# Batch 0's first row half multiplied unfolded, and its scores in two tiles: a chunked attention followed by a Fourier mixing layer on one core

## The chip, the core and the metric

The kernel runs on one core of one Trainium2 chip. The metric is the device time of one execution in microseconds (us). Three runs of the kernel before took 282.17, 284.47 and 280.91, median 282.17. A separate, profiled execution is what all views of the profile below come from.

## The reference

Two layers, for 4 batches of 768 positions, 8 heads of 64 (512 columns):

```python
for c in range(nc):                               # chunks of 32 queries
    k_ctx = k[:, :, l_start:r_end]                # 16 keys to the left, 8 to the right
    k_full = np.concatenate([mem_k, k_ctx], axis=2)   # and 8 memory keys; v alike
    scores = scale * np.matmul(q_c, k_full.transpose(0, 1, 3, 2))
    a = softmax(scores)
    out[:, :, c_start:c_end] = np.matmul(a, v_full)
x = out.transpose(0, 2, 1, 3).reshape(B, S, H * D)
mixed = np.real(fft(fft(x, axis=1), axis=2))      # over 768 positions, then 512 columns
u = x + mixed
un = (u - mean(u)) / sqrt(var(u) + 1e-06)
return u + np.maximum(un @ w_ch1, 0.0) @ w_ch2    # 512 -> 2048 -> 512
```

`softmax` stands here for the reference's maximum, exponential and division.

## The kernel before

**Who orders the work.** The program is a list of tasks. Each `add(engine, cost, emit, after, take, give, ...)` names an engine, a cost in us, the tasks it comes after and the buffers it takes and gives back. `Plan.order()` walks a clock of its own over this list, picks for each engine the first task in rank whose conditions hold, and emits the instructions in that order. The order is thus fixed when the program is built; on the chip each engine works strictly in it and waits on semaphores. While the first scores are due, the planner puts small matmuls on a zero tile (`idle`, L902) where it sees TensorE without work; until `WARM` it counts TensorE's costs double.

**Attention.** A pair of heads is one unit n; `seq` gives 4 pairs for each of 4 batches (n = 0 to 15). For each n, GpSimd's queue loads queries and keys into one of three stages (`qs`, `ks`, L349; for batch 3 L345), SP's queue loads the values in seven pieces into one of four tiles `va` (L358, L362, L367). TensorE turns queries and keys (`trq`, `trk`, L377, 16 matmuls each), ScalarE copies the turned queries (L395), VectorE in batch 0 and ScalarE later copies the keys into `kTb` (L420), and TensorE computes scores in two halves g = 0, 1 of 12 matmuls (`sc`, L433). All score halves share one PSUM tile `sc`: the second half can be computed when ScalarE's exponential of the first (L441, two instructions, into one of three tiles `e`) has read it. The value products follow (`xa`, `xo`, L457), with the softmax sum as a column of their own, and VectorE divides into `xsb` (L467, L468). The first 32 rows of each `va` are zeroed on ScalarE (L331, 1.5 us each). A copy named `gate` (L956, GpSimd) reads a value of the last pair of batch 0, second head, and thereby holds the loads of batch 1 behind that transfer.

**Fourier layer.** It is a product with cosine and sine tables. Rows first: the columns are folded so that only sums and differences are multiplied. For batches 1 to 3 (`fourier`, L529) all six row tiles come at once. For batch 0 (`first_fourier`) the work is done in two row halves g: g = 0 as soon as the first three row tiles of all four pairs are there. VectorE adds and subtracts column halves (`zy`, L599), folds them twice (`ff`, L610, for g = 0; `g_w` and `g_both`, L616 and L635, for g = 1), ScalarE rounds to f16 (`hi`, L651), VectorE takes the remainder (`lo`, L655), and TensorE multiplies with the tables (`ps`, L688, 12 matmuls for each of four column parts (par, ab) and each half). One column that the folding leaves over is multiplied by itself (`mid`, L675, after a matmul with zeros, L669, that opens its tile). Each finished part is copied by ScalarE and VectorE in two f16 pieces (`up`, L541, L546). Then the column products (`pm`, L699), the sum with the input (L705), mean and variance (L713, L714), the normalised tile (`un`), its turn (`tp`, L730, in batch 0) and the two layers.

**Layers.** `ph` (L775) is layer 1, in groups of 8 matmuls, with the relu on ScalarE (L784). `pc` (L793) is layer 2 for batches 0 and 1, and L842 with half the width, with fewer products, for batches 2 and 3. The weights come on GpSimd's queue (`w_sb`, L1062 for layer 1, L1067 for layer 2). TensorE's order interleaves the layers of one batch with the attention of the next.

PSUM: tags `acc` and `mlp` have two banks each, `tr`, `sc` and `xa` one each.

Of the kernel before, what the change touches and what calls it, by code (L numbers as in the profile page):

```python
# [10 lines left out]
FP32 = mybir.dt.float32  # L11
BF16 = mybir.dt.bfloat16
# [24 lines left out]
class Plan:  # L37
# [4 lines left out]
    LAG = {"PE": 0.2}  # L42
    FIRST = 45.0
    WARM = 18.0
    SLACK = 0.7
    FILL = 0.17
# [44 lines left out]

    def order(self):
        now, idle = 0.0, {}
        self.flow, self.seen = {}, 0.0
# [6 lines left out]
        placed = []  # L101
        while any(waiting.values()):
# [5 lines left out]
            for e, ts_ in waiting.items():  # L108
                if idle.get(e, 0.0) > now:
                    continue  # L110
                held = False
                for t in ts_:
# [29 lines left out]
                    idle[e] = t["end"] = now + cost  # L142
                    if t["moved"]:
                        self.flow.setdefault(e, []).append([t, t["moved"], now + cost * t["head"]])
                        self.share(now)
                        t["end"] = t["done"]
                    else:
# [10 lines left out]
                else:  # L158
                    if e == "PE" and self.filling and self.filling[0]["at"] is not None \
                            and self.filling[1]["at"] is None:  # L160
                        cost = self.FILL * (2.0 if now < self.WARM else 1.0)
                        idle[e] = now + cost
                        placed.append(dict(engine="PE", cost=cost, emit=self.fill, at=now,
                                           done=now + cost))
                        moved = True
            if not moved:
                times = ([v for v in idle.values() if v > now] + [g[0] for g in gives]
                         + [t["done"] + x for t in placed for x in (0.0, self.SLACK, 4.0, 8.0)
# [9 lines left out]
def kernel(  # L178
# [38 lines left out]

    bank_of, bank_free = {}, {"acc": [0, 1], "mlp": [0, 1]}

    def bank(tag, shape, dtype, name):  # L220
        i = bank_free[tag].pop(0)
        t = fps.tile(shape, dtype, tag=f"{tag}{i}", bufs=1, name=name)
# [14 lines left out]
    ks = [spool.tile([P, 2, RB * D], BF16, name=f"ks{i}") for i in range(NS)]  # L237
    NV = 4
# [43 lines left out]
    odd = wpool.tile([P, 2, 3, NK], FP16)  # L282
    cosD = wpool.tile([P, 2, HD], FP16)
# [45 lines left out]
    def e_low_rows(i):  # L329
        low = va[i][0:MEM0].rearrange("p h t c -> p (h t c)")  # L330
        nc.scalar.copy(low, zero[0:MEM0].to_broadcast([MEM0, 2 * NT * 66]))  # L331
# [8 lines left out]
    def e_load_qk(n, i):  # L340
        b, pr = seq[n]
        src, dst = ((q, qs), (k, ks))[i]
        if b >= TURNED:
            for hh in range(2):
                nc.gpsimd.dma_start(  # L345
                    strided(dst[n % NS], hh * D, [[2 * D, NST], [1, D]]),
                    src[b, 2 * pr + hh].rearrange("(a p) d -> p a d", p=P))
            return
        nc.gpsimd.dma_start(dst[n % NS][0:QP],  # L349
# [30 lines left out]
    def e_flip_q(n):  # L380
        qT_of[n] = qT = apool.tile([P, S], BF16, tag="qT", bufs=2, name="qT")
        nc.sync.dma_start_transpose(qT.rearrange("p (a s) -> p a s", s=P),
                                    qs[n % NS].rearrange("p h c -> p (h c)")[:, 0:S])

    def e_flip_k(n):
        nc.sync.dma_start_transpose(kU[n % NKU][:, KR:KR + S].rearrange("p (a s) -> p a s", s=P),
                                    ks[n % NS].rearrange("p h c -> p (h c)")[:, 0:S])
# [1014 lines left out]
```

## Time and profile before

| what | value |
|---|---|
| profiled execution, own time | 282.55 us |
| its span | 280.7 us |
| median of the three runs | 282.17 us |
| TensorE busy | 264.3 us (94%) |
| VectorE, ScalarE, GpSimd busy | 193.5, 155.2, 64.3 us |
| granted TensorE clock | 1.00 throughout |
| share of the chain that ended last | TensorE 84%, DMA 7%, VectorE 4%, SP's queue 3% |
| first layer-1 matmul | at 57.1 us |
| last TensorE instruction ends | at 277.5 us |

The page gives busy times by engine, and the span in 40 slices whose digits are tenths of busy time. PE is TensorE, PEld its weight loads, DVE is VectorE, ACT ScalarE, POOL GpSimd, SP the queue that issues most transfers. L numbers are lines of the kernel. In a timeline each row has the start, the duration, the engine, the line, the operation, and in brackets the idle time before it with what ended it. Matmuls overlap each other, so that a row's duration is longer than the step from one to the next; steps are read from start to start.

### The profile page before, as it was taken

The numbers are of one execution on the slowest core, as the hardware profiler recorded it, in microseconds if no ns is written. First come the engines' busy times: TensorE is split into PE (matmuls) and PEld (weight loads), VectorE is DVE, ScalarE is ACT, GpSimd is POOL, SyncE is SP. The second block draws the span as 40 slices with busy tenths as digits, with TensorE's granted clock in tenths as the row PEclk, the third lists the DMA queues.
The fourth block names the chain that finished last, engine by engine and source line by source line (L and its number), as shares of the span: only waits on it lengthen the run. The fifth ranks groups of instructions, "written<-read, shape, count | busy, mean of one in ns | idle before, by whom it ended". The sixth has DMA issues, their size and how long they took to land.

```text
span 280.7 us, 7981 instructions
## 1 busy us (share of the span) xinstructions
PE 264.3 (94%) x3325; PEld 207.4 (74%) x3325; DVE 193.5 (69%) x424; ACT 155.2 (55%) x262; POOL 64.3 (23%) x127
## 2 busy tenths in 40 slices
PE   0589999999999999998999999999999999999995
PEld 0466698788756579766668766858988888888884
DVE  7968978970218979899688776599869825353444
ACT  6887667579665757734745665525526270605150
POOL 8840853240111038306200230101004100000000
PEclk9999999999999999999999999999999999999999
DMA  6989999999899969999999734497101507103152
GB/s 102 199 143 174 162 206 204 196 198 201 162 190 236 214 103 220 177 142 144 235 191 209 177 74 109 108 207 167 48 37 58 131 21 168 40 37 77 50 103 76
DMA packets 116116, 39.98 MB, mean 142 GB/s; under 512 B 104560, under 2 KB 111472, under 8 KB 116080
## 3 DMA queue, kind: packets, MB, share of 16 engines
q1 hardware_dynamic: 93888, 23.54, 46.9%
q0 software_dynamic: 21472, 15.21, 34.0%
q10 hardware_dynamic: 720, 0.72, 0.7%
q8 instruction: 26, 0.43, 0.7%
q14 instruction: 10, 0.08, 0.1%
HBM read 37.36 MB, written 13.37 MB: 181 GB/s over the span
## 4 chain that ended last, share of the span: by engine, by line
PE 84%; DMA 7%; DVE 4%; SPq 3%; issue 1%; POOL 0%; POOLq 0%
PE ph L775 31%; PE pc L793 15%; PE pc L842 13%; DMA va<-in_v_dram 6%; PE ps L529 6%; PE xa L457 4%; PE pm L699 4%; PE ps L688 3%; PE xo L457 3%; PE sc L433 2%; SPq L358 2%; DMA qs<-in_q_dram 1%; PE trk L377 1%; PE trq L377 1%; DVE xsb L705 1%; PE pm L580 1%
## 5 line engine op out<-in xcount | busy, mean ns | idle before, releaser
L775 PE MATMUL ph<-unT,w_sb 128*128 128x256 f16 x768 | 90.3, 273 | 0.8 <-DVE xsb L800 0.8
L784 ACT ACTIVATE hT<-ph 128x512 f16<-128x512 f32 x96 | 56.9, 598 | 54.3 <-PE pc L842 30.2
L775 PEld LDWEIGHTS <-w_sb 128*128 128x128 f16 x768 | 73.2, 98 | 11.1 <-issue 1.7
L793 PE MATMUL pc<-w_sb,hT 128*128 128x512 f16 x192 | 44.8, 380 | 0.0
L441 ACT ACTIVATE e<-sc,mbias 128x384 f32<-128x384 f32 x64 | 33.6, 576 | 19.0 <-PE sc L433 19.0
L793 PEld LDWEIGHTS <-hT 128*128 128x128 f16 x192 | 17.7, 98 | 19.0 <-issue 0.2
L847 DVE TENSOR_TENSOR xsb<-pc,xsb 128x256 f32<-128x256 f32 x43 | 18.0, 421 | 12.4 <-PE pc L842 10.6
L842 PEld LDWEIGHTS <-hT 128*128 128x128 f16 x240 | 23.3, 98 | 4.2 <-DVE hT L830 1.0
L842 PE MATMUL pc<-w_sb,hT 128*128 128x256 f16 x192 | 24.1, 272 | 0.5 <-DVE hT L830 0.5
L541 ACT CAST up<-ps 128x386 f16<-128x386 f32 x16 | 9.7, 605 | 17.6 <-PE ps L529 17.0
L830 DVE TENSOR_TENSOR S<-hT 128x768 f16<-128x768 f16 (+1 forms) x12 | 5.1, 422 | 18.5 <-ACT hT L784 17.9
L800 DVE SCALAR_TENSOR_TENSOR xsb<-pc,rstd,xsb 128x512 f32<-128x512 f32 x12 | 9.0, 750 | 12.2 <-PE pc L793 12.1
L713 DVE BATCH_NORM_STATS2 st<-xsb 128x6 f32<-128x512 f32 x24 | 16.6, 690 | 0.6
L705 DVE TENSOR_TENSOR xsb<-pm,xsb 128x512 f32<-128x512 f32 x15 | 10.2, 678 | 7.1 <-PE pm L699 6.9
L457 PEld LDWEIGHTS xa<-va,e 128*64 128x64 f32 x384 | 12.5, 137 | 3.2 <-issue 2.0
L457 PE MATMUL xa<-va,e 128*64 128x65 f32 x384 | 14.7, 226 | 0.0
L433 PEld LDWEIGHTS <-kTb 64*128 64x128 bf16 x384 | 7.8, 96 | 9.0 <-issue 8.1
L457 PE MATMUL xo<-va,e 128*64 128x65 f32 x384 | 14.1, 223 | 0.0
L546 DVE TENSOR_TENSOR up<-ps,up 128x386 f16<-128x386 f32 x16 | 9.6, 602 | 6.1 <-ACT up L541 6.1
L395 ACT COPY qT<-trq 128x768 bf16<-128x768 bf16 x12 | 9.5, 793 | 6.4 <-PE trq L377 6.4
L572 POOL DMA_DIRECT2D xr<-x_back x3 | 2.3, 770 | 46.7 <-DMA x_back<-x_rows 46.7
L519 DVE TENSOR_TENSOR lo<-ff,hi 128x768 f16<-128x768 f32 x12 | 11.3, 954 | 2.4 <-ACT hi L514 2.4
(168 smaller groups left out, 455.3 us busy)
## 6 DMA issues: line engine op xcount, KB each, us to landing
va<-in_v_dram SPq DMA_DIRECT2D x32, 220.0 KB
w_sb<-in_moe_w_ch_dram POOLq DMA_DIRECT2D x8, 512.0 KB, 16.9
out_dram<-xsb SPq DMA_DIRECT2D x12, 256.0 KB
qs<-in_q_dram POOLq DMA_DIRECT2D x12, 192.0 KB, 6.5
ks<-in_k_dram POOLq DMA_DIRECT2D x12, 192.0 KB, 7.0
x_rows<-xsb POOLq DMA_DIRECT2D x3, 768.0 KB, 4.6
xr<-x_back POOLq DMA_DIRECT2D x3, 768.0 KB, 5.0
out_rows<-xsb SPq DMA_DIRECT2D x9, 256.0 KB
```

The costliest lines, as they stand in the source:

```text
L433: nc.tensor.matmul(sc[:, hh, t6, :], kT[r0:r0 + 64, t, :], qT[r0:r0 + 64, ts(t, 64)], start=True, stop=True, tile_position=(r0, 0))
L441: nc.scalar.activation(e1[:, :, :, ts(half, 32)], sc[:, :, 0:6, ts(half, 32)], AFT.Exp, bias=mbias[:, half:half + 1], scale=1.0 / math.sqr ...
L457: nc.tensor.matmul(xa[64 * half:64 * half + 64, st, hh, 0:65], e1[:, hh, t6, :], v1[:, hh, 6 * g + t6, 0:65], start=True, stop=True)
L519: nc.vector.tensor_tensor(lo[:, ab].rearrange(fl), ff_of[b, par][:, ab].rearrange(fl), hi[:, ab].rearrange(fl), ALU.subtract)
L529: nc.tensor.matmul(out_[:, sp, :], part[:, ab, sp * 3 + st, c0:c1], tab[:, sp, st, :], start=(st == 0 and i == 0), stop=(st == 2 and i == 1))
L705: nc.vector.tensor_tensor(uv, pm_of[b, kt], uv, ALU.add)
L713: nc.vector.bn_stats(st6, xs[b][:, kt, :])
L775: nc.tensor.matmul(ph[:, k, :], w1_sb[:, dt, ts(HH * k + i, P)], unT_of[b, j][:, dt, :], start=(dt == 0), stop=(dt == NDT - 1))
L784: nc.scalar.activation(hT_of[b, j][:, :, i, :], ph, AFT.Relu, bias=0.0, scale=1.0 if b in EVEN else -1.0)
L793: nc.tensor.matmul(pc_of[b, j, r], hT_of[b, j][:, k, i, ts(r, P)], w2_sb[:, HH * k + i, :], start=(i + k == 0), stop=(i + k == HH))
L842: nc.tensor.matmul(pc_of[key], a[:, i, :], w[:, i, :], start=(i == 0 and new), stop=(i == HH - 1), skip_group_check=not new)
L847: nc.vector.tensor_tensor(u, pc, u, ALU.add)
```

## The change

Batch 0's first row half (g = 0) is no longer folded at the second level. Its column half `zy` and a reversed half (`g_back`) are each rounded and multiplied (`g_rows0`, two passes `back` = 0, 1), the second pass partly with negated tables (`odd`, and `neg`, new, in the buffer `S`). The second half (g = 1) stays folded and is added to the same PSUM sums; the left-over column of both halves is combined on GpSimd and multiplied once at the end (`g_mid`, `g_row`). The score tile of g = 1 in batch 0 is half of a new two-bank tile `accs` from a pool that is given back before the first `acc` bank is used; two of the four row sums sit in the `sc` tile. The fourth pair has a stage of its own (`last_qk`). Two of the `va` tiles are zeroed on GpSimd. The planner's costs are changed, `WARM` is 6, its filling matmuls use any of three tags and give them back, and it makes 24 orders with randomly moved ranks and keeps the one that ends first by its own clock. Values of n = 14, 15 are issued after the turned rows of batch 2; layer 2's weights go out after n = 7. Keys of n = 5, 6, 7 are copied by VectorE.

```diff
-    WARM = 18.0
+    OVER = {"DVE": 0.08, "ACT": 0.1}
+    WARM = 6.0
+    ROOM = 2.2
...
+    def shortest(self, tries, spread):
+        ...
+        for i in list(range(tries)) + [None]:
+            draw = random.Random(found[1] if i is None else i)
+            ...
+            for t, rank in zip(self.tasks, ranks):
+                move = draw.gauss(0.0, spread)
+                t["rank"] = rank if even or rank < self.lead or rank > 1e5 else rank + move
...
+            placed = self.order()
+            if found is None or self.end < found[0]:
+                found = (self.end, i)
+        return placed
...
+                        tag = next((x for x in ("mlp", "tr", "xa") if self.free[x] > 0), None)
...
+    early = tc.tile_pool(name="early_ps", bufs=1, space=bass.MemoryType.PSUM)
+    accs = [early, early.__enter__().tile([P, 2, 512], FP32, name="accs")]
...
+        if tag == "acc":
+            if len(accs) == 2:
+                early.__exit__(None, None, None)
...
+    last_qk = wpool.tile([P, 2, 2, RB * D], BF16, tag="w2t", bufs=1, name="last_qk")
...
+    neg = fpool.tile([P, 2, 3, NK], FP16, tag="S", bufs=1, name="neg")
...
-        nc.scalar.copy(low, zero[0:MEM0].to_broadcast([MEM0, 2 * NT * 66]))
+        if i < 2:
+            nc.scalar.copy(low, zero[0:MEM0].to_broadcast([MEM0, 2 * NT * 66]))
+        else:
+            nc.gpsimd.memset(low, 0.0)
...
+    KDVE, QDVE = (5, 6, 7), ()
...
-        if n < HP:
-            trk = bank("acc", [P, RB * KP], BF16, "trk")
+        tr_of[n, 1] = trk = (bank("mlp", [P, RB * KP], BF16, "trk") if n < HP else
...
-        sc_of[n, g] = sc = aps.tile([P, 2, 8, 64], FP32, tag="sc", bufs=1, name="sc")
+        sc_of[n, g] = sc = (accs[1].rearrange("p h (t q) -> p h t q", q=64) if n < HP and g == 1 else
+                            aps.tile([P, 2, 8, 64], FP32, tag="sc", bufs=1, name="sc"))
...
-    def g_ff(par, ab, g, last):
...
+    def g_back(par):
+        ff_of[0, par] = fpool.tile([P, 2, NST, P], FP32, tag="fold", bufs=2, name="ff0")
+        xb = xs[0][:, 0:3]
+        nc.vector.tensor_tensor(ff_of[0, par][:, 0, 0:3, 1:P],
+                                rev_ap(xb, 2 * P - 1, P - 1, [[DM, 3]]),
+                                rev_ap(xb, 2 * P - 1 + HD, P - 1, [[DM, 3]]),
+                                ALU.add if par == 0 else ALU.subtract)
...
+    def g_edge2():
+        hi, lo = (g_hl(1, i)[:, 1, 0:3, 0] for i in range(2))
+        nc.gpsimd.tensor_copy(hi, mid32[:, 0:3, 0])
+        nc.gpsimd.tensor_tensor(lo, mid32[:, 0:3, 0], hi, ALU.subtract)
+
+    def g_rows0(par, ab, back):
+        if not back:
+            if par == 0:
+                if ab == 0:
+                    g_of["ps"] = aps.tile([P, 2, 8, 64], FP32, tag="sc", bufs=1, name="ps")
+                ps_of[0, par, ab] = strided(g_of["ps"][:, ab], 0, [[NK, 2], [1, NK]])
+            else:
+                ps_of[0, par, ab] = bank("acc", [P, 2, NK], FP32, "ps")
+        ps = ps_of[0, par, ab]
+        for sp in range(2):
+            tab = ((neg, odd)[sp][:, ab] if back and ab != par else (cosS, sinS)[ab][:, sp])
+            for st in range(3):
+                for i in range(2):
+                    nc.tensor.matmul(ps[:, sp, :], g_hl(par, i)[:, back, st, :], tab[:, st, :],
+                                     start=(not back and sp + st + i == 0), stop=False)
...
-            ps_of[0, 0, 1] = bank("acc", [P, 2, NK], FP32, "ps")
-            nc.tensor.matmul(ps_of[0, 0, 1].rearrange("p s k -> p (s k)"), dz,
-                             strided(dz, 0, [[0, NK], [1, 2]]), start=True, stop=False)
...
-                nc.gpsimd.tensor_copy(gate[64:65], va[n % NV][64:65, 1, NT - 1, 0:1])
+                nc.gpsimd.tensor_copy(gate[64:65], va[n % NV][64:65, 0, NT - 1, 0:1])
...
-            if b == 1 and i in (1, 2):
+            if b == 1 and i in (1, 3):
                 weights(b * HP + i)
...
+    t_lv[14]["behind"] = t_x2[TURNED - 1]
+    t_lv[15]["behind"] = t_x2[TURNED - 1]
+
     with tc.manual_schedule():
-        for t in plan.order():
+        for t in plan.shortest(24, 1.5):
             t["emit"]()
```

In TensorE's new order, batch 0 stands so: 17 fillers, then turns, fillers and scores with both halves of a pair together, the four pairs of value products, 84 unfolded row matmuls, 24 folded, 12 unfolded, 12 for the left-over column, 24 folded; then the query turn of n = 4 and the columns, with the key turn and the scores of n = 4 and the turns of n = 5 between them, and the first group of layer 1 before the value products of n = 4. Before, the value products of n = 4 and 5 and the scores of n = 5 stood ahead of that group.

## The prediction

> **What bounds the kernel now.** I read the page first, then the windows view cut where the kernel changes character, then the timelines of TensorE, ScalarE and GpSimd up to 57 us, and last the chain that ended last. The page:
>
> ```profile
> span 280.7 us, 7981 instructions
> PE 264.3 (94%) x3325; PEld 207.4 (74%) x3325; DVE 193.5 (69%) x424; ACT 155.2 (55%) x262; POOL 64.3 (23%) x127
> PE   0589999999999999998999999999999999999995
> DMA  6989999999899969999999734497101507103152
> ```
>
> TensorE is busy nearly everywhere except in the first two slices (7 us each). The windows (stretch, its length, then busy time and instructions of PE, PEld, DVE, ACT, POOL, the granted clock, DMA share, GB/s) say where that is real:
>
> ```profile
> 0.00:31.70 31.70, 20.90 (x443) 14.98 (x443) 26.38 (x74) 23.76 (x40) 18.87 (x51) 1.00 0.96 155
> 31.70:57.10 25.40, 24.36 (x414) 21.05 (x409) 22.10 (x53) 15.61 (x29) 10.85 (x21) 1.00 1.14 196
> 57.10:277.60 220.50, 219.09 (x2478) 171.41 (x2474) 144.60 (x299) 115.83 (x193) 34.56 (x56) 1.00 0.78 135
> 277.60:280.70 3.10, 0.00 (x0) 0.00 (x0) 0.38 (x1) 0.00 (x0) 0.00 (x0) 1.00 0.32 111
> ```
>
> From 57.1 us, where the first layer-1 matmul (ph) starts, TensorE stands idle for only 1.4 of 220.5 us: there a matmul saved or added is a matmul's time saved or added, and nothing else counts. Before that it is different. Of the 20.9 us "busy" up to 31.7 us much is filling: the attention of batch 0 needs only 12.2 us of TensorE (4 query turns of 0.46, 4 key turns of 0.47, 8 score halves of 0.28, 4 pairs of value products of 1.55). The timeline of TensorE shows what it waits for there:
>
> ```profile
> 14.61 1.46 PE L902 MATMUL idle<-dz 128*128 128x384 bf16 x4
> 24.16 1.15 PE L902 MATMUL idle<-dz 128*128 128x384 bf16 x6
> 27.13 0.35 PE L433 MATMUL sc<-qT,kTb 64*128 64x64 bf16 x12
> 28.26 0.82 PE L902 MATMUL idle<-dz 128*128 128x384 bf16 x4
> 29.01 0.35 PE L433 MATMUL sc<-qT,kTb 64*128 64x64 bf16 x12
> 29.29 0.92 PE L457 MATMUL xa<-va,e 128*64 128x65 f32 x24
> 30.90 0.92 PE L457 MATMUL xo<-va,e 128*64 128x65 f32 x24
> ```
>
> and ScalarE and GpSimd beside it:
>
> ```profile
> 27.58 1.05 ACT L441 ACTIVATE e<-sc,mbias 128x384 f32<-128x384 f32 x2 [0.83 <-PE sc L433]
> 29.47 1.05 ACT L441 ACTIVATE e<-sc,mbias 128x384 f32<-128x384 f32 x2 [0.56 <-PE sc L433]
> 27.44 0.47 POOL L956 COPY gate<-va 1x1 f32<-1x1 f32 x1 [9.63 <-DMA va<-in_v_dram]
> ```
>
> With one score tile a score half and its exponential take turns: 1.88 us from score to score (27.13 to 29.01) for 1.05 us of exponential. The fourth pair's values land at 27.4 (the gate copy waits for them), yet its second product ends only at 31.7. So the start has two limits close together, the loads of V and the score-exponential chain, and the chain is the later one by about 2.7 us (27.4 + 0.05 + 1.55 = 29.0 would be possible).
>
> From 31.7 to 57.1 TensorE has real work: rows of the transform, columns, turns, two more pairs of attention. The chain gives the prices:
>
> ```profile
> 33.50 1.10 PE ps L675 x12
> 35.07 3.13 PE ps L688 x36
> 48.48 0.70 DVE xsb L705
> 57.16 1.85 PE ph L775 x16
> ```
>
> A column block ends in VectorE's sum (48.48), which returns later. A row matmul (L688) costs 3.13/36 = 0.087 us, one for the single middle row (L675) 1.10/12 = 0.092.
>
> **The account.** Time = start of the first ph + TensorE's work after it + its waits after it + the tail + what lies around the span. Before: 57.1 + 217.4 + 3.1 + 3.1 + 1.85 = 282.55, the profiled execution's own time (span 280.7). The 217.4 are counts by steps (ph 0.109, layer 2 0.2155, half-width layer 2 0.109, later row transforms 0.0845, columns 0.11, the attention prices above, 0.1 for each return from attention to f16 work). The median of the runs shown, 282.17, lies 0.4 lower. Each part of the change is put into these terms.
>
> **Row transform of batch 0.** Removed: 96 matmuls of L688, 24 of L675 and one zeroing matmul (about 0.3): 8.35 + 2.2 + 0.3 = 10.85 us. Added: 96 unfolded and 48 folded row matmuls and 12 for the middle row, by the same steps, 12.5 + 1.1 = 13.6. TensorE's work grows by 2.8 us, and because it is work ahead of a saturated stretch nothing hides it. VectorE loses eight folds (L610, 0.55 each, 4.4) and gains two (1.1) and two negated tables (0.4 each): 2.5 less. GpSimd gains small edge operations of 0.2 to 0.5 each, between the query loads and the weights; they hold the last twelve unfolded matmuls, which the order puts behind 24 others (2.1 us) as cover.
>
> **Scores in two tiles, stages, fillers.** Two limits again. Loads: the same bytes must land before the fourth pair's values. The fourth pair's queries and keys get a stage of their own, so GpSimd issues them near 9.3 instead of 16.5, into a stretch that is full up to 14 and then slack (DMA share 0.59 and 0.29 in the two microseconds from 15). That can win up to 1.5 us; against it, V's first two pairs now share with them and the gate reads the first head's values, so batch 1's queries and keys start while the second head's still come. Bounds for the landing: 26 and 29.5; I take 28.0, nearest to the row at 27.4 with the earlier gate against it. The chain: the first exponential comes later than now (13.74), near 15.3, because ScalarE first copies the second pair's queries and twenty fillers stand among the first turns; then 8 exponentials of 1.05, two copies of 0.8, one cast of 0.5 and about 1.5 of waits for the three e tiles make 27.7, which just meets the loads. So the last value product ends at 28.0 + 1.55 = 29.6 (bounds 27.5 and 33) instead of 31.7.
>
> A word on the fillers, 54 instead of 29, with 17 in one run at the start. The trace shows two steps for them: 1.46/4 = 0.365 at 14.6 and 1.15/6 = 0.19 at 24.2, while the granted-clock column reads 1.00 at both, so the column does not show it. I take 0.19 from 6 us on; the other end is 0.365 up to about 17, as now. [...] By the rows alone it stays open.
>
> **From there to the first ph.** 29.6 + 13.6 of row matmuls (VectorE's folds, by the list of its instructions, run 0.3 to 1 us ahead of each block) = 43.2; the last row's copy on ScalarE 0.6, its rest on VectorE 0.6 and 0.2 of hand-over: 44.6. Then the columns: 48 matmuls 5.25, 12 turns 0.65, one query and two key turns 1.4, two score halves 0.55 = 7.85, and 0.8 of waits for VectorE's sums (now 9.7 us pass between 47.46 and 57.16 for 8.5 of work, 1.2 of waits). First ph at 53.25, or 3.85 earlier than 57.1.
>
> **But less has been done by then.** In the old order two pairs of values (3.1), two more score halves (0.55) and one more query turn (0.45) stood before the first ph; now they stand behind it, and with them four more returns at 0.1. TensorE's work after the first ph is 217.4 + 4.5 = 221.9.
>
> **The rest of the order.** Values of batch 3's last two pairs are queued on SP behind the turned rows of batch 2; by the new order their products stand some 50 us of TensorE work behind the last attention product of batch 2, so the load's 5 us and the turn's 6 are covered; without that cover each would cost its wait. Layer 2's weights go out after the last pair of batch 1 instead of the third, and layer 2 comes 25 us after the first ph. The zeroing of two value tiles moves from ScalarE (1.5 each) to GpSimd; nearest row, 1024 elements in 1.03 us, gives 1.6 each, and behind it stands only the gate. Three key copies go from ScalarE to VectorE (1.04 to 1.23 each), both with idle time there. One of 24 orders is chosen by the planner's own costs: it can remove at most what TensorE waits now (1.4 idle, 3.1 with the small hesitations), and can add waits; bounds -1.5 and +3, taken 0.
>
> **Sum.** 53.25 + 221.9 + 3.1 + 3.1 + 1.85 = 283.2; against the median 0.4 lower: 282.8. The start wins 3.85, the extra matmuls and the postponed attention take 4.5 back.
>
> **Rivals.** (1) *The loads pack better*: slack at 15 to 17 is used fully, values land at 26, the exponentials run without waits for the e tiles, and the rest loses its hesitations: -2.1 - 1.5 gives 279.2. For it: the DMA share there. Against it: V's own pace later, 4.7 us a pair with little beside it (76.5 to 81.2, and the next ones). (2) *The slower side: fillers at the long step.* If TensorE falls back during the wait for the first turn and steps long from 8.7 to 16.4 us, as it does now, half of these 7.7 us is lost, 3.85; as the engine works in order, scores, exponentials and the last value product slip from the 28.6 that the chain alone gives (27.7, half a pair and the hand-over) to 32.5, 2.9 behind my 29.6. It decides once the second pair's scores start after 19.5 us. Price 2.9: 285.7. For it: turns at 0.85 for 16 up to 14 us now; against it: the seventeen fillers ahead. (3) *The new order stalls later*: a block waits for VectorE in batch 1 or 2, as now at 128.09 (0.8), two to four times: 285. (4) *It doesn't do what it says*: the second score tile brings nothing because the loads end last anyway, at 29.5; then 284.5.
>
> **How the numbers follow.** The forecast, within 1.5 us of 282.8: 0.52. Rival 1: 0.16; rival 2: 0.12; rivals 3 and 4 together 0.20. Two per cent (5.6 us) is about what a measurement here can tell from no change. Rival 1 reaches beyond that with a third of its chance; rival 2 does where a stall of rival 3 comes on top, half of it, and 3 on 4 with a third: faster 0.05, slower 0.13, within 0.82. The range takes in rivals 1 to 4 and a stall of 1 us on top of rival 2: 279.2 to 287.2; the forecast's own is 281.3 to 284.3.
>
> **What would show it.** Right: score halves of one pair back to back (0.56 for 24), the last value product ending near 29.6, one block of 156 row matmuls of 13.6 us, the first ph near 53, TensorE idle under 3 us after it. Wrong: values of the fourth pair landing before 25 or after 30; fillers at 0.36 after 9 us; gaps of over 0.5 us in the row block; a first ph before 50 or after 56; or TensorE's work after the first ph not near 222.

## The result, and the profile after

The changed kernel takes 292.75 us (median of 4 executions, 290.36 to 294.40) against 283.32 (280.91 to 284.57) of the kernel before: ratio 1.0353, 95% interval 1.0304 to 1.0402. It is slower by 3.5%; 282.8 was forecast. The profiled execution took 293.36 us, 10.81 more than the one of before. First its page, then the windows view (stretch, its length, busy time and instructions of PE, PEld, DVE, ACT, POOL, granted clock, DMA share, GB/s), cut as before at the last value product, the first ph and the last matmul:

```profile
span 291.6 us, 8093 instructions
PE 276.2 (95%) x3385; PEld 213.3 (73%) x3385; DVE 196.1 (67%) x423; ACT 149.5 (51%) x254; POOL 69.1 (24%) x136
PE   7779779999999999999999979999999999999995
PEclk9797999999999999999999999999999999999999
```

```profile
0.00:38.30 38.30, 29.46 (x472) 18.33 (x473) 25.97 (x72) 21.73 (x35) 22.48 (x59) 0.91 0.85 148
38.30:61.36 23.06, 22.71 (x305) 20.11 (x304) 18.87 (x41) 11.98 (x24) 11.09 (x20) 1.00 1.01 187
61.36:288.50 227.14, 224.05 (x2614) 174.89 (x2610) 150.85 (x310) 115.78 (x195) 35.52 (x57) 1.00 0.75 130
288.50:291.60 3.10, 0.00 (x0) 0.00 (x0) 0.42 (x1) 0.00 (x0) 0.00 (x0) 1.00 0.35 119
```

The first stretch is where it went: it ends at 38.3, where the forecast had 29.6 and the kernel before 31.7, and its mean clock is 0.91. The second is as forecast (23.1 us; 23.65 in the sum). The third is 227.1 + 3.1 = 230.2 us long, 2.1 more than the 228.1 of the sum. TensorE's timeline in the first stretch, and VectorE, GpSimd and ScalarE beside it:

```profile
1.04 5.36 PE L980 MATMUL idle<-dz 128*128 128x384 bf16 x17 [1.04 <-DVE zero L339]
8.79 0.23 PE L1107 MATMUL mps<-ident_b,mkb 128*128 128x128 bf16 x1 [2.38 <-DVE mkb L1101]
8.85 1.68 PE L980 MATMUL idle<-dz 128*128 128x384 bf16 x6
11.25 2.12 PE L980 MATMUL idle<-dz 128*128 128x384 bf16 x7
13.30 0.55 PE L429 MATMUL trk<-turn_b,ks 100*64 100x100 bf16 x16
15.20 0.70 PE L980 MATMUL idle<-dz 128*128 128x384 bf16 x3 [0.33 <-DVE kTb L471]
16.56 0.35 PE L485 MATMUL sc<-qT,kTb 64*128 64x64 bf16 x12
21.23 0.48 PE L980 MATMUL idle<-dz 128*128 128x384 bf16 x2 [1.45 <-DVE kTb L471]
22.54 0.35 PE L485 MATMUL sc<-qT,kTb 64*128 64x64 bf16 x12
24.06 1.53 PE L509 MATMUL xa<-va,e 128*64 128x65 f32 x24
38.08 0.27 PE L509 MATMUL xo<-va,e 128*64 128x65 f32 x1 [3.07 <-issue]
```

```profile
17.23 1.60 DVE L1133 TENSOR_SCALAR nsinD<-sinD 128x512 f16<-128x512 f16 x1
19.99 1.18 DVE L471 COPY kTb<-trk 128x1056 bf16<-128x1056 bf16 x1
17.27 2.91 POOL L383 MEMSET va<- 32x1584 f32 x2
24.55 0.18 POOL L1039 COPY gate<-va 1x1 f32<-1x1 f32 x1 [2.84 <-DMA va<-in_v_dram]
31.64 1.05 ACT L493 ACTIVATE e<-accs,mbias 128x384 f32<-128x384 f32 x2
```

The gate, which now reads the first head's values, passes at 24.55, yet the last exponential ends at 32.7, 5 us behind the 27.7 of the forecast, and the last value product 8.7 us behind its 29.6. Fillers stand ahead of the first key turn (13.30; 9.79 before) and of the second pair's scores (22.54; 17.65 before); twice a filler itself waits for a key copy (0.33, 1.45). The second key copy stands behind the table row nsinD, which takes 1.60 us beside GpSimd's zeroing where it took 0.37 before. The first value group takes 1.53 us instead of 0.92, and at 35 TensorE stands 3.07 us with nothing shown that it waits for. Cutting the clock's column finer, here of TensorE alone, gives two stretches at half rate (9.41 to 12.82 and 23.06 to 26.48):

```profile
9.40:12.80 3.40, 3.40 (x25) 0.50 1.32 202
23.00:26.50 3.50, 3.50 (x67) 0.51 0.61 101
```

There is a third slow stretch that the column does not show. The first 17 fillers take 5.36 us together, 0.32 each, where a filler takes about 0.18 at whole clock (24.16 to 25.24 for six, in the kernel before); the column reads 1.00 there, and so does the kernel before's "1.00 throughout" over its fillers of 0.35 (14.61 to 16.00 for four).

Behind the first ph there is one new wait. In order: GpSimd's scale of batch 2 and behind it the issue of the mirrored rows, VectorE's wait for these rows, TensorE's wait for VectorE:

```profile
162.02 0.23 POOL L815 TENSOR_SCALAR rs<-mu_s 128x2 f32<-128x2 f32 x1 [15.33 <-DVE zs L519]
163.91 0.87 POOL L625 DMA_DIRECT2D xr<-x_back  x1 [0.25 <-issue]
171.20 0.69 DVE L640 TENSOR_TENSOR xsb<-pm,xr 128x510 f32<-128x510 f32 x1 [1.80 <-DMA xr<-x_back]
172.00 0.38 PE L778 MATMUL pm<-cosD,up 128*128 128x256 f16 x2 [1.62 <-DVE xsb L642]
```

### The profile page after: what moved, and what is told of

Same layout as the page of the kernel before. It is cut to its first block, busy times and chain, and to the rows that moved or that the text cites. A ratio compares the mean times of both kernels' runs of the same rounds, so it can differ in the third digit from the quotient of the medians.

```text
span 291.6 us, 8093 instructions
## 1 busy us (share of the span) xinstructions
PE 276.2 (95%) x3385; PEld 213.3 (73%) x3385; DVE 196.1 (67%) x423; ACT 149.5 (51%) x254; POOL 69.1 (24%) x136
## 4 chain that ended last, share of the span: by engine, by line
PE 79%; DVE 11%; issue 3%; DMA 2%; ACT 2%; POOL 0%; POOLq 0%; DVEq 0%; ACTq 0%
PE ph L854 23%; PE pc L872 15%; PE pc L921 11%; PE ps L581 5%; PE xa L509 4%; PE pm L778 4%; PE xo L509 3%; PE idle L980 3%; PE sc L485 3%; DMA xr<-x_back 2%; PE ps L702 2%; PE trq L429 2%; PE trk L429 2%; ACT un L803 1%; PE ps L759 1%
## 5 line engine op out<-in xcount | busy, mean ns | idle before, releaser
L872 PE MATMUL pc<-w_sb,hT 128*128 128x512 f16 x192 | 45.5, 380 | 0.0
L493 ACT ACTIVATE e<-sc,mbias 128x384 f32<-128x384 f32 x56 | 29.5, 581 | 17.6 <-PE sc L485 14.9
L980 PE MATMUL idle<-dz 128*128 128x384 bf16 x54 | 16.4, 415 | 3.3 <-DVE kTb L471 1.8
L803 ACT ACTIVATE un<-xsb,rs 128x512 f16<-128x512 f32 x12 | 9.4, 808 | 16.3 <-POOL rs L818 16.3
L509 PE MATMUL xo<-va,e 128*64 128x65 f32 x384 | 14.7, 227 | 3.1 <-issue 3.1
L509 PEld LDWEIGHTS xa<-va,e 128*64 128x64 f32 x384 | 13.2, 143 | 4.7 <-issue 3.7
L909 DVE TENSOR_TENSOR S<-hT 128x768 f16<-128x768 f16 (+1 forms) x12 | 5.1, 424 | 16.1 <-ACT hT L863 15.5
L509 PEld LDWEIGHTS xo<-va,e 128*64 128x64 f32 x384 | 13.3, 143 | 3.2 <-issue 3.2
L509 PE MATMUL xa<-va,e 128*64 128x65 f32 x384 | 15.3, 232 | 0.1
L519 DVE RECIPROCAL zs<-xa 128x6 f32<-128x6 f32 x16 | 3.0, 188 | 16.6 <-PE xa L509 16.5
L815 POOL TENSOR_SCALAR rs<-mu_s 128x2 f32<-128x2 f32 x6 | 1.3, 223 | 50.0 <-DVE mu_s L793 34.6
```

Of the source, the lines that this page charges most:

```text
L493: nc.scalar.activation(e1[:, :, :, ts(half, 32)], sc[:, :, 0:6, ts(half, 32)], AFT.Exp, bias=mbias[:, half:half + 1], scale=1.0 / math.sqr ...
L509: nc.tensor.matmul(xa[64 * half:64 * half + 64, st, hh, 0:65], e1[:, hh, t6, :], v1[:, hh, 6 * g + t6, 0:65], start=True, stop=True)
L803: nc.scalar.activation(un, xs[b][:, kt, :], AFT.Identity, bias=rs[:, 1:2], scale=rs[:, 0:1])
L872: nc.tensor.matmul(pc_of[b, j, r], hT_of[b, j][:, k, i, ts(r, P)], w2_sb[:, HH * k + i, :], start=(i + k == 0), stop=(i + k == HH))
L980: nc.tensor.matmul(idle[:, 0:384], dz, strided(dz, 0, [[0, 3], [1, P]]), start=True, stop=True)
```

## The experiments

In all of them the order that the planner chose is written out once and then edited, so that nothing else moves (warm_18 and no_draws alone let the planner make another order):

```
placed = plan.shortest(24, 1.5)
...                       # the edit
for t in placed: t["emit"]()
```

All but the first run replace the 26 transposing DMAs (batches 1 to 3) by plain copies of the same bytes; that transposition is left out. before_plain, below, prices this.

**Mirrored rows issued first**

```
+placed.insert(placed.index(scales[0]), placed.pop(placed.index(t_xr[2])))
```

> The changed kernel with its planned order kept, but on GpSimd's queue the issue of batch 2's mirrored rows stands ahead of the first scale of batch 2 instead of behind it. Later-waits theory (the issue at 163.91 waits behind a scale that waits for VectorE until 162.02, while the rows have been back since about 154): the issue moves to 154 to 156 us, TensorE's wait of 1.62 us at 172.0 and the wait of 0.84 at 182.5 go, time 2.0 to 2.5 us under 292.75, ratio 1.027 to 1.028. Rival: another wait takes the place (the scale itself, 175.98, stays late for its own statistics): less than 0.7 us, ratio above 1.033.

290.1 us, ratio 1.0255 (1.0217 to 1.0293). The issue now stands at 152.93:

```profile
152.93 0.76 POOL L625 DMA_DIRECT2D xr<-x_back  x1 [9.79 <-DMA x_back<-x_rows]
```

The 1.62 us wait is gone; the other, expected to go from 182.5 too, stays (0.73 us instead of 0.84). From the first ph to the end it is 228.4 us instead of 230.2: 1.8 us, a little under what was expected. The rest of the difference to 292.75 is the start's scatter: here the clock stayed whole at 23 us and the wait at 35 was 0.82 us, with the same order.

**Control**

```
-nc.sync.dma_start_transpose(...)      +nc.sync.dma_start(...)
```

> The control for the start's experiments: the changed kernel, with its 26 transposing DMAs (batch 1 to 3's normalized rows, batch 3's q and k) made plain copies of the same bytes; the transposition is left out, nothing of batch 0 is touched. All theories: the start is that of the changed kernel (first scores 16.56, second key copy 19.99, first value group at 23.6 to 24.1, first ph between 57.5 and 61.4), the time 289 to 294, a little less than the changed kernel's if the transposes' arrivals held TensorE somewhere. Two things may differ from run to run with the same order: whether the clock falls to a half after TensorE's idle time at 19.8 to 21.2 (it did in the changed kernel's profile, from 23.06, and not in that of the mirror edit) and how long TensorE stands at about 35 without a wait shown (3.07 and 0.82 us). The code theory says of the second: each such gap ends just after a packet of TensorE's code has landed (36.56 for the gap that ended at 38.08; 31.88 + 0.95 = 32.83 for the one that ended at 34.31).

290.27 us is the median, but the four executions lie far apart: 284.04, 288.48, 292.06 and 292.08, with mean granted clocks of 1.000, 0.993, 0.982 and 0.976. Only the lowest kept its clock whole, so no ratio is given, and every difference to 290.27 below holds only within some us. The profiled one (292.08) has two half-clock stretches, 8.2 to 15.0 and 21.8 to 28.6, and VectorE's table steps show the other thing at work:

```profile
17.05 1.61 DVE L1130 TENSOR_SCALAR neg<-sinS 128x579 f16<-128x579 f16 x1
18.57 1.60 DVE L1127 TENSOR_SCALAR odd<-cosS 128x579 f16<-128x579 f16 x1
20.09 1.70 DVE L1127 TENSOR_SCALAR odd<-sinS 128x579 f16<-128x579 f16 x1
17.01 2.99 POOL L383 MEMSET va<- 32x1584 f32 x2
24.47 0.80 PE L980 MATMUL idle<-dz 128*128 128x384 bf16 x2 [3.60 <-DVE kTb L471]
```

Each of these steps takes 0.31 us in the changed kernel (15.28 to 15.72); here each ends as a zeroing on GpSimd ends (the third under the zeroing of kU, from 20.07), the key copy behind them starts at 23.23, and a filler waits 3.60 us for its bank; the copy was expected at 19.99. The mirrored rows are issued as late here (164.11) as in the changed kernel, and still TensorE does not wait:

```profile
169.90 0.69 DVE L640 TENSOR_TENSOR xsb<-pm,xr 128x510 f32<-128x510 f32 x1 [0.30 <-DMA xr<-x_back]
```

With plain copies the rows arrive 5.8 us after their issue instead of 7.3. So the late issue costs its 1.8 us only together with the slower arrival.

**No later fillers; table rows late; both**

```
+for t in placed[placed.index(t_mps):]:          # first edit
+    if "rank" not in t: t["emit"] = no_fill
+placed.insert(late_of, placed.pop(placed.index(t_rows)))   # second
```

> The control without the 37 filler matmuls that stand behind the memory keys' transpose (the 17 ahead of it stay). Fillers theory (they stand in TensorE's order and push the first turns and scores back; two of them wait 0.33 and 1.45 us for a bank that a key copy reads): the first key copy starts at 11.5 instead of 13.89 us, the first scores at 13.5 to 14 instead of 16.56, and the first ph comes 2 to 4 us before the control's; time 2 to 4 us under the control's. VectorE theory (the second key copy stands behind the table rows, which run under GpSimd's zeroing): the rows still stand ahead of the second copy but start 2.5 us earlier and miss the zeroing, so that the 1.60 us of the first of them falls to about 0.37; if they still run at 17 us, the copy ends at 21 as before and less than 0.5 us is won. Clock theory: TensorE has longer idle stretches without fillers, the granted clock falls to a half in some of them and the value products stay at 1.4 to 1.5 us a group instead of 0.9, which takes back 1 to 3 us.

> The control with the task of the table rows (the 512-wide negation and its 8 one-row memsets on VectorE) moved from ahead of the second key copy to behind the lower parts of batch 0's first row half. VectorE theory: the second key copy starts at about 18.0, at the end of its turn, instead of 19.99; TensorE's idle time from 19.77 to 21.23 shrinks under 0.5 us and the clock has no reason to fall; scores and values come 2.0 us earlier, first ph 2 us before the control's if that keeps its clock and 3 to 3.5 if not; time 2 to 3.5 us under the control's. Fillers theory alone: the scores are late through TensorE's own order, less than 0.7 us comes back. Code theory: the gap at 35 depends on when code arrives, which this edit does not touch; it stays at 0.8 to 3 us.

> The control with both edits: without the 37 later fillers, and with the table rows behind the first half's lower parts. If fillers and table rows are two causes in a row, the gains add: first key copy at 11.5, second at about 15.5, first value group at 20 to 21, last value product bounded by the values' arrival (gate at 24.6) near 29 to 30, first ph at 54 to 56, time 4 to 6 us under the control's. If one of them is the whole cause, this equals the better of the two alone within 1 us. If the loads set the end, first ph stays within 1 us of the control's whatever the order.

Without the 37 fillers: 282.17 us, ratio 0.9997 (0.9971 to 1.0024), 8.1 under the control's median. Without the control the price comes out smaller: mirror_first (290.1, the same start) less the 1.4 us that plain copies are worth in the kernel before gives 288.7, and 6.5 for the fillers. Against the control's one execution with a whole clock (284.04) it is 1.9. With the rows moved: 286.73, 1.0146 (1.0088 to 1.0203). With both: 282.16, 0.9991 (0.9967 to 1.0015), no better than the first alone. TensorE without later fillers:

```profile
9.31 0.52 PE L429 MATMUL trk<-turn_b,ks 100*64 100x100 bf16 x16
17.57 0.50 PE L485 MATMUL sc<-qT,kTb 64*128 64x64 bf16 x12 [2.08 <-DVE kTb L471]
27.23 0.93 PE L509 MATMUL xa<-va,e 128*64 128x65 f32 x24 [0.70 <-DMA va<-in_v_dram]
```

The fourth pair now waits for its values (27.23), so the loads end the start; its last product ends at 28.9 and the first ph comes at 51.88. Against the control's median the table rows cost 3.5 us, but only while the fillers stand with them: without, the second key copy still waits for them, but the wait falls into the slack ahead of the loads. The clock is at a half from 10.4 to 20.6 in this run, and what that costs falls into the same slack.

**Fillers in other banks, and the planner's constant put back**

```
+t["emit"] = fill_acc if i < scored else fill_xa      # filler_banks
-WARM = 6.0    +WARM = 18.0                           # warm_18
```

> The control with all its fillers, but those ahead of the first value product write banks that no other engine reads at that time: the second score tile before the first scores, the value bank after them, instead of the banks that key copies read. It tells the two ways apart in which fillers hold up TensorE's order. Time theory (a filler takes 0.25 to 0.33 us here where the plan counts 0.17, and 20 of them stand ahead of the first scores: 1.55 + 2.26 + 1.79 us of fillers between the transpose and the second query turn): the first key copy still starts at 13.9, first scores at 16.2 (only the 0.33 us wait goes), and the second pair's scores still wait for a key copy that ends at 21; at most 2 us under the control's 290.3, so 288 to 290. Bank theory (the waits of 0.33 and 1.45 to 3.6 us for a key copy's bank are what makes it late): near the 282.2 of the run without later fillers, below 285.

> The control with one constant of the planner put back: the time up to which it counts TensorE's work double is 18 us as in the kernel before, not 6. Fillers then count 0.34 us in the start, and 8 of them stand behind the transpose of the memory keys instead of 37; the order of everything else follows the plan. Filler theory: the price of a filler in the plan is what let the start slip; first key copy 12 to 12.5, first value group before 21, first ph at 52 to 54, time 282 to 285. VectorE theory: the table rows still stand ahead of the second key copy in VectorE's order, but run at 13 to 14 us, before GpSimd's zeroing; no difference to the filler theory here. Rival (the start is slow whatever the fillers, the run without them had only luck with the clock): above 288.

With other banks: 286.99, 1.0152 (1.0098 to 1.0206), 3.3 under the control's median, between the two theories: no filler waits any more, and its first key copy starts at 13.76. With the constant back: 282.51, 1.0001 (0.9955 to 1.0048). That one number, by which the planner counts a filler at 0.34 us up to 18 us instead of 0.17 from 6 us on, decides nearly all of the start, though the order behind it changes with it: 8 later fillers instead of 37, first ph at 52.55.

**The idle time ahead of the fillers closed**

```
+placed[at:at] = [dict(engine="PE", emit=e_fill) for _ in range(8)]   # at: t_mps
```

> The control with 8 more fillers ahead of the memory keys' transpose (25 instead of 17), which fill the 2.1 to 3.3 us in which TensorE stands idle before 8.79. All else is the control's, its 37 later fillers too. Clock theory (what the fillers cost is mostly that the clock is halved some 0.6 to 1.7 us after that idle time, so that 13 fillers and two turns take 5.5 to 6.7 us instead of 4.2): the half-clock stretch at 8 to 15 us goes, the first key copy starts at 12.5 or before as in the run that kept its clock (12.49), the first ph comes at 55 or before, time 284 to 286. Order theory (that they stand in TensorE's order ahead of work at all): the copy still comes 0.9 us or more after 11.6, and the time stays at least 3 us above the 282.2 of the run without later fillers. If neither the idle time nor the clock matters, 288 to 292 as the control.

> The run without later fillers, with the 8 more ahead of the transpose. If the clock stays whole through the start (in the run without later fillers it was halved from 10.4 to 20.6), turns take 0.53 instead of 0.85 to 0.88 and the first value groups 0.9 instead of 1.53; if the start were set by TensorE's own order, the last value product would come 1.5 to 2 us earlier and the time fall to 280.5. Load theory (the fourth pair's product waits for the values' arrival: 0.70 us at 27.2): first ph within 0.5 us of 51.9 and the time within 0.5 us of 282.2.

With all later fillers: 284.57, 1.0101 (1.0046 to 1.0156). Without them: 282.14, 0.9994 (0.9974 to 1.0015). In the first the clock reads 1.00 in all five windows of TensorE from 5 to 38.3 us (its four executions have means of 0.998 to 1.000), and the first key turn starts at 11.89:

```profile
9.40:12.80 3.40, 3.34 (x45) 1.00 1.30 213
```

```profile
11.89 0.54 PE L429 MATMUL trk<-turn_b,ks 100*64 100x100 bf16 x16
```

45 matmuls where the changed kernel ran 25. More fillers make the kernel 5.7 us faster than the control's median, and as fast as the control's one execution with a whole clock (284.04). So of the 8.1 us some 5.7 hang on the clock (4 of the 6.5 counted without the control), and 2.4, bridge against bridge_no_later, are the fillers' place in the order. Without later fillers nothing is won, as the load theory said, though its condition was not met in full: the clock still fell, from 12.0 to 22.3, after TensorE's idle time from 9.83 to 11.28. The second key copy comes 0.9 us earlier (15.44 instead of 16.33), and the values are still waited for until 27.45.

**Zeroing back on ScalarE**

```
-nc.gpsimd.memset(low, 0.0)     +nc.scalar.copy(low, zero...)    # behind t_exp[0, 1]
```

> The control with its fillers, but the two 32-row zeroings of the third and fourth value tile run on ScalarE behind the first pair's exps, where it is idle, instead of on GpSimd at 17.0 to 20.1 us. Nothing else is moved: the table rows still stand ahead of the second key copy on VectorE. Overlap theory (VectorE's SBUF-to-SBUF table work stands still while GpSimd zeroes: in the control three such steps took 1.60 to 1.70 us each and in the changed kernel one 1.60, against 0.30 without a zeroing beside it): all of them take 0.4 us or less, the second key copy starts at 18.0 to 19.5 instead of 19.99 to 23.2, and the time is 286 to 288, like the run with the rows moved (286.7). Rival (the long steps come from the order or from a lower clock): the steps stay at 1.2 us or more and the time at 289 to 291.

288.42, 1.0224 (1.0195 to 1.0252); by time not decided. The steps in its profile:

```profile
13.66 1.26 DVE L1130 TENSOR_SCALAR neg<-cosS 128x579 f16<-128x579 f16 x1
14.84 0.33 DVE L1130 TENSOR_SCALAR neg<-sinS 128x579 f16<-128x579 f16 x1
15.83 0.29 DVE L1133 TENSOR_SCALAR nsinD<-sinD 128x512 f16<-128x512 f16 x1
13.80 0.95 POOL L964 MEMSET ks<- 4x1024 bf16 x1
```

All but one are short; the one that is not lies under another memset of GpSimd, and ends just after it. But this profiled execution (285.33) kept a whole clock, and the rows ran at 13.66 to 16.1, ahead of 17.0, where the zeroing stood: moving it was not put to the test. What decides are two traces with the same step at the same time beside the same memset, first without later fillers, then with the 8 more ahead (bridge_no_later):

```profile
13.97 1.20 DVE L1133 TENSOR_SCALAR nsinD<-sinD 128x512 f16<-128x512 f16 x1
14.04 0.95 POOL L964 MEMSET ks<- 4x1024 bf16 x1
```

```profile
13.97 0.31 DVE L1133 TENSOR_SCALAR nsinD<-sinD 128x512 f16<-128x512 f16 x1
14.04 1.13 POOL L964 MEMSET ks<- 4x1024 bf16 x1
```

One of the two is held up, once VectorE until the memset ends, once GpSimd. In all 17 traces every one of these table steps over 0.45 us lies beside a memset of GpSimd of over 0.7 us and ends at most 0.2 us after one; with no such memset beside them they take 0.27 to 0.40. The overlap is what makes them long, and neither the order nor the clock does.

**What the other parts are worth without the fillers**

```
-sc = accs[1]... if g == 1 else aps.tile(...)   +sc = aps.tile(...)    # one_score_tile
+for t in t_back: t["emit"] = lambda: None                             # no_back_products
-placed = plan.shortest(24, 1.5)                +placed = plan.order() # no_draws
```

> The run without later fillers, with both score halves in the one tile of before; the order is kept, so each second half waits for the exponential of the first. It prices the second tile. If the score and exponential chain is the limit that the second tile lifted, each pair loses 0.8 to 1.3 us, the last value product comes 2 to 4 us later, and the time rises to 284 to 286. If the values' loads end last anyway, less than 1 us: 282 to 283.

> The run without later fillers, and without the 48 matmuls of the first row half's mirrored pass (their part of the row sums is left out, and nothing else). Count theory (TensorE runs from the last value product to the columns without a wait there, so that the unfolding costs what its matmuls take): first columns 4.0 to 4.2 us before 43.05, first ph at 47.8, time 278 to 278.5, ratio about 0.985 to 0.987. VectorE theory (the second row half's lower parts come no earlier than now): TensorE waits for them where the 48 stood, and less than 2 us is won: 280.5 to 282.

> The run without later fillers, with the plan's plain order instead of the shortest of 24 drawn ones. Batch 0's tasks are not moved by the draws, so the start is the same: first ph at 51.9 within 0.3. If the draws found an order that is shorter on the chip, this is slower than 282.2 by 0.5 to 2 us; if they only suit the plan's own prices, within 0.7 us of it or faster.

One score tile: 290.89, 1.0301 (1.0246 to 1.0355), 8.7 us worse. TensorE's waits from 8 to 40 us name it (total, times, longest):

```profile
PE sc L485 <- ACT e L493: 6.0, 4, 2.1
```

That is more than the 284 to 286 expected; part of it goes with a clock at a half from 8.3 to 25.3 and 28.8 to 35.6 in its profile. So in this order, which was made for two tiles, the second tile is what lets the loads end the start. No mirrored products: 282.62, 1.0003 (0.9952 to 1.0055), no gain, against 4 us by count. TensorE waits instead:

```profile
PE ps L766 <- DVE up L598: 1.3, 1, 1.3
PE ps L759 <- ACT hi L737: 1.2, 1, 1.2
PE ps L759 <- DVE lo L740: 0.5, 1, 0.5
```

3.0 of the 4.2 us come back as waits for the second half's parts; 1.2 us reach the first ph (50.64) and 1.0 the end of the profiled execution (281.04 against 282.00), but not the median of four that lie between 281.04 and 283.86. No draws: 288.79, 1.0218 (1.0159 to 1.0278), 6.6 us worse, with the first ph at 52.69, 0.8 later than expected. TensorE waits once for a normalized row (timeline), and then the clock falls (windows, 0.51):

```profile
130.32 2.44 PE L854 MATMUL ph<-unT,w_sb 128*128 128x256 f16 x16 [2.24 <-DMA unT<-un]
```

```profile
131.50:138.50 7.00, 5.91 (x30) 3.97 (x29) 6.86 (x13) 4.57 (x8) 4.58 (x4) 0.51 0.75 204
```

The 8 layer-2 matmuls ahead of it and the 48 of layer 1 behind it took 13.35 us from start to next start (126.19 to 139.54), where the steps of the account give 1.72 + 5.24 = 6.96: a wait of 2.2 us, with what followed it, cost 6.4. This wait is for one of the plain copies; with the transposing DMAs it was not tried.

**The kernel before, with plain copies, with and without fillers**

```
-for t in plan.order(): t["emit"]()
+for t in plan.order():
+    if "rank" in t: t["emit"]()
```

> The kernel before, with its 26 transposing DMAs made plain copies of the same bytes (the transposition is left out), to see what the control's edit alone is worth. If TensorE never waits for a transposed tile in the kernel before (its waits behind the first ph add up to 0.8 us), the time is that of the kernel before within 0.8 us: ratio 0.997 to 1.0. If the transposes' share of the DMA engines held something up, up to 2 us less, and then the runs of the control series have to be read 2 us higher against the kernel before.

> The kernel before with plain copies, and without its 25 fillers behind the first one. Its fillers stand at 13.4 to 30.9 us, 4 or 6 in a row ahead of scores and values. Fillers theory: where one of them still runs when the next real work is ready, 0.1 to 0.8 us a place is lost, at up to 7 places; last value product at 30 instead of 31.7 and 1 to 2 us less than the plain run of the kernel before, which would make this faster than both kernels. Clock theory: without them TensorE's clock falls to a half in the waits at 24 to 31 us, where in the kernel before it stayed whole; the row products that follow take 1.5 times as long for some us, and the time is 1 to 3 us over the plain run. If the loads alone set this start, within 0.5 us.

Plain copies alone: 280.95, 0.9951 (0.9936 to 0.9967); the transposes cost 1.4 us, more than I had allowed. Where is open: in the profiles 1.0 us of it lies ahead of the first ph (56.13 against 57.09), where no transposing DMA runs yet, and 0.1 behind it. Without fillers: 280.73, 0.9945 (0.9926 to 0.9965), the same: the first ph comes 1.3 us later in its profile, after a half-clock stretch from 31.4 to 34.8, and what follows is 0.8 shorter. The few fillers of the kernel before are worth about what they cost. Measured with the same copies, the changed kernel without its later fillers (282.17) is still 1.2 us slower than the kernel before. No edit of the changed kernel here is clearly faster than the kernel before.

## Why the prediction was wrong

**The failing step is the word on the fillers.** It took 0.19 us a filler from 6 us on; no trace of the changed kernel or of the control shows that term. In the changed kernel TensorE stood idle for 2.38 us ahead of the first turn, the clock fell at 9.41, and the next 13 fillers took 0.27 to 0.29 us each (8.85 to 10.46 and 11.25 to 13.30), or 0.34 in the control, where the clock was at a half all through them. In zeroing_on_scalar, whose clock stayed whole there, the same 13 took 0.20 each (8.86 to 10.03 and 10.50 to 11.90). The two steps it read off the rows (0.365 and 0.19) are durations shared out; from start to start they are 0.35 and 0.18, so the slow one was sized about right and the wrong one was taken. Rival 2 was the right one, and its sign was met (second pair's scores at 22.54, beyond 19.5), but it was priced at 2.9 us. The fillers cost 6.5 to 8.1, shown by taking them away. What the price left out: a filler that waits for a key copy's bank holds all of TensorE (3.60 us in the control; 3.3 us under the control's median with banks alone changed); the late first copy moves VectorE's table steps under GpSimd's zeroing (1.60 us instead of 0.3); the clock fell a second time, at 23.06, after TensorE's idle time from 19.77 to 21.23; and the code wait told below. They overlap and do not add up: 4 to 5.7 us go with the clock alone.

Of the clock the traces show this much. Its half-clock stretches last 3.41 us in the changed kernel (both), 6.8 in the control (both), 10.2 without later fillers and 17.0 for the longer one with one score tile. Idle time alone does not decide a fall: 2.38 us of it was followed by the fall at 9.41, 1.45 us by the one at 23.06, while zeroing_on_scalar stood idle for 3.27 us ahead of 8.79 and kept its clock. TensorE's order alone does not either: with the same order the first fall came at 9.41 in the changed kernel and at 8.2 in the control, and at 23 us the clock was at a half in the changed kernel and whole in mirror_first. What decides it stays open.

**"Behind it stands only the gate."** The zeroing's price was right (2.91 us for two, 3.2 forecast), its cover was not looked up on the other engine: beside it VectorE's table steps take 1.6 us instead of 0.3. The steps above end as the zeroing ends, and in bridge_no_later the memset is the one held up (1.13 instead of 0.95 us). Why the two hold each other up, no run shows.

**Loads and chain: right, once the fillers are gone.** The fourth pair's values were taken to land at 28.0; TensorE waits for them until 27.2. The last value product was to end at 29.6: 28.9 without later fillers. Rival 4, that the second tile brings nothing, is wrong in this order, by up to 8.7 us.

**Row block to first ph: right.** From the last value product to the columns 15.0 us forecast, 14.2 measured; to the first ph 8.65 forecast, 8.8 measured. But "nothing hides it" was not right for the added products: without the 48, TensorE waits 3.0 us for VectorE and ScalarE.

**TensorE's work behind the first ph: right.** 228.1 with waits and tail in the sum; 228.4 in mirror_first and without later fillers. The 230.2 of the changed kernel is rival 3's kind, one block that waits for VectorE, 1.8 us; an earlier issue on GpSimd's queue removes it, and so do plain copies.

**The draws at 0.** Against the kernel before it holds; but the plain order would have cost 6.6 us in the plain-copy runs, so the 0 was luck in part: the draws won back about what the plain order loses.

**The sum.** The forecast says that the extra matmuls and the postponed attention take 4.5 us back. By its own terms the 4.5 are the postponed attention alone; the 2.8 of extra matmuls are already inside the 3.85 that the start wins. The total is not touched by that. With what the runs took away it closes: 292.75 - 8.1 - 1.8 = 282.85, the forecast's 282.8. The 8.1 is a difference to a median that scatters by some us, and the plain copies are not counted, so the agreement is better than it deserves.

## What to carry to other kernels

A filler is work in the order of its engine: price it at the clock that holds when it runs (0.18 to 0.20 us at a whole clock here, 0.34 at a half), keep it off banks that another engine reads (a wait of 3.60 us in the control), and either close the idle time ahead of it (284.57 us with 8 more) or leave it out (282.17). A start whose real limit is a load, as here without later fillers (a wait of 0.70 us for the values at 27.23), has slack for slow matmuls, and fillers eat that slack first. When a step moves to another engine, look at what else runs on both engines at that moment (table steps of 1.6 us instead of 0.3 here), not only at what is queued behind it.

## What the runs showed of the hardware

The profile lists a DMA queue q8 of the kind "instruction": 26 packets of 16 KB, 0.43 MB together, in the changed kernel, and as many in the kernel before. That they are the code of TensorE's 6770 matmuls and weight loads is a reading of mine that no run shows. One of them, seen in the DMA view of the changed kernel between 35.2 and 36.6 us (packets, MB, share):

```profile
q8 instruction: 1, 0.02, 5.6%
```

This packet landed at 36.56 and TensorE went on at 38.08, 1.52 us later, after its 3.07 us of waiting for nothing shown. In mirror_first the wait of 0.82 us ended 1.48 us after a packet's landing (32.83 to 34.31). Two other traces have such a wait, 1.31 us up to 33.28 (rows_late) and 1.19 us up to 32.15 (zeroing_on_scalar). All four have the 37 later fillers; three others with them have no such wait, and none of the seven with 8 or none. That the code was late is argued from these times; what decides when a packet is asked for stays open, and no run changed the code's size alone.
